# Other planning figures for the attention steps of a fused RWKV and tanh-shrink kernel

## The chip, the cores and the metric

The kernel runs on one core of a Trainium2 chip. A core has five engines that run their own instruction queues in order and wait for each other through semaphores: TensorE (PE, matrix products), VectorE (DVE), ScalarE (ACT), GpSimd (POOL) and SyncE (SP, here only for issuing transfers). The metric is the device time of one execution in microseconds; smaller is better.

## What is computed

Two blocks follow each other. The first is a linear attention with a decaying state; the second a two-layer block with the activation h - tanh(h). All numbers are 32-bit floats as the kernel computes them.

```python
for t in range(S):                       # B, H, S, D = 4, 8, 768, 48
    kt, vt, rt = k[:, :, t], v[:, :, t], r[:, :, t]
    cur = np.einsum('bhd,bhe->bhde', u[None] * kt, vt)
    y[:, :, t] = np.einsum('bhd,bhde->bhe', rt, state + cur)
    state = w[None, :, :, None] * state + np.einsum('bhd,bhe->bhde', kt, vt)
...
x = y.transpose(0, 2, 1, 3).reshape(B * S, H * D)     # 3072 x 384
h = x @ w_in                                          # w_in 384 x 2048
g = h - np.tanh(h)
return g @ w_out                                      # w_out 2048 x 384
```

## The kernel before

**Attention in units.** A unit is 64 time steps of two batches with all heads; there are 24 units, and two neighbouring units make one block of 256 tokens for the dense part (12 blocks). A unit consists of these steps, with their names in the code:

- `x.turn` and `x.turn_k` (line 763, PE): eight transposes each of r and of k into PSUM (the banks that products are written to). From unit 2 on, what is turned for k is `kw`, which DVE makes first (`x.kw`, line 894).
- `x.rT` (line 767, DVE) and `x.kT` (line 776, ACT, for later units): copies out of PSUM, r scaled by powers of the decay.
- `x.rk`, its product with `ub`, and `x.du` (lines 780, 909, 784, DVE), then `diagonal` (line 788, ACT, eight small copies): the part of each step's own key.
- `from_state` and `levels` (line 717, PE): products of rT with the state, and of rT with kT. In the first 16 units both are one planned step; in the last eight (`two`) they are two, with a tiny ACT copy `seen` (line 816) between them.
- `x.cp` (line 919, DVE): a masked copy of the levels from PSUM into `at`.
- `outputs` and `to_state` (line 717, PE): products of `at` with v, and of kw with v.
- `x.xt` and `x.rest` (line 855, ACT): copies of the result into the dense part's input, negated for every second unit; then six transfers `fill` on POOL's queue (line 876) that move the rest of the rows to their place.
- `x.add` and `x.decay` (lines 882 and 928, DVE): the new state.

**The dense part in tiles.** A tile is one block of 256 tokens and 256 of the 2048 inner columns. PE makes two halves of h (line 168, six matmul records each); ACT makes five functions of it (lines 177 to 185); DVE combines them into g (lines 192, 194, 196 and 198, the last being the masked copy that ends g). Then comes the second product. For the first 24 tiles it is taken directly (`o`, line 206); later seven products of quarter size replace eight (`p`, line 257), from sums of g that POOL makes (lines 242 to 246) and from mixed weights that DVE makes once (`mixed`, line 266). The first six blocks are taken in three passes over the inner columns (4, 4 and 8 pieces of 128), the other six each in one.

**Weights.** They arrive as 64-bit numbers in 16 pieces (line 123, on SP's and POOL's queues) and are turned into 32-bit ones by five DVE steps (lines 137, 138, 141, 142, 143) and two ACT steps (139, 140).

**What sets the order.** Nothing is issued where it stands in the source. Each step is handed to `Plan.add` with its engine, a cost in us, the steps it has to wait for, and `steps`, the number of engine instructions it stands for. `Plan.order` then looks for an order: `forward` plays all queues through with these costs, `backward` gives latest times, and a search with a fixed random seed changes due times, 2500 times with the work done by 240 us as its aim and 500 times with the whole length, and keeps what the planner finds no worse. The instructions of every engine are issued in the order of the last plan kept. In `forward`, `steps` are counted in chunks of 256 instructions, for which a load of instructions is assumed, and PE's idle time before the first dense work is filled with matmuls of the identity (line 655, `fills`), whose number follows from the planned gaps. Each change of a figure therefore moves the results of comparisons in the search, and with them the order of all queues.

The planner's figures are used for nothing else: they change neither an instruction nor what it waits for.

Of the kernel before, what the change touches and what calls it, by code (L numbers as in the profile page):

```python
# [300 lines left out]
class Plan:  # L301
# [15 lines left out]
    def add(self, engine, cost, run, after=(), due=1e9, data=0, gated=False, steps=0):  # L317
        t = SimpleNamespace(engine=engine, cost=cost, run=run, after=[x for x in after if x], due=due, data=data,
                            gated=gated, steps=steps, then=[], n=len(self.tasks))
        for x in t.after:  # L320
            x.then.append(t)
        self.tasks.append(t)
        return t
# [192 lines left out]
def near(ctx, tc, r, k, v, w, u, out, shared, moe_w_in, moe_w_out):  # L516
# [21 lines left out]
    add = plan.add  # L538
# [114 lines left out]
    def fills(to):  # L653
        def run(n):
# [6 lines left out]
    now = [add(e, 1.25 if e == "ACT" else .87, lambda e=e, at=at, x=x: e_of[e].dma_start(out=rows[at : at + NP, :, :D], in_=x.rearrange("(p i) d -> p i d", i=2)), due=-1, data=.05)  # L661
           for e, at, x in (("SP", 0, w), ("ACT", NP, u))]
# [3 lines left out]
    now = add("DVE", .45, lambda: V.tensor_scalar(  # L666
        by[:, :, 1:], wcol[:, :, None].to_broadcast([128, NP, SHORT]), W_LOW, W_HIGH, ALU.max, ALU.min), [cols])
    now = add("DVE", .7, lambda: V.tensor_tensor_scan(
        power.rearrange(flat), by.rearrange(flat), plus.rearrange(flat), 0.0, ALU.mult, ALU.add), [now])

    ups = add("ACT", .6, lambda: A.copy(w_up, power[:, :, None, :SHORT].to_broadcast([128, NP, 2, SHORT])), [now])
    now = add("DVE", 1.75, lambda: V.reciprocal(inverse, power), [now])
    inverted = now
    doubled = add("ACT", .6, lambda: A.copy(twice, inverse[:, :, None, 1:].to_broadcast([128, NP, 2, SHORT])), [now])
    now = tabled = add("PE", .7, table, [doubled], steps=8)
# [3 lines left out]
    now = add("POOL", 1.0, bounds, [keeps])  # L679
    now = add("PE", .2, lambda: T.matmul(tab[0:1, 0:1], ok[:, 0, :1], shared["one"], start=True, stop=True), [now, downs])  # L680
# [20 lines left out]
    for n in range(weights.count):  # L701
# [8 lines left out]
        now = of + ([converted[n - 2]] if n >= 2 else [])  # L710
        for name, cost in (("DVE", .47), ("DVE", .47), ("ACT", .84), ("ACT", .84), ("DVE", .87), ("DVE", .87), ("DVE", .87)):
            now = [add(name, cost, step, now)]
# [8 lines left out]
    def unit(n):  # L721
# [3 lines left out]
        ch, half = divmod(n, 2)  # L725
# [4 lines left out]
        two = n >= L * (FIRST + 2)  # L730
# [5 lines left out]
        b1, b2, b3 = (units[n - i] if n >= i else none for i in (1, 2, 3))  # L736
        x = SimpleNamespace(rest=None, rk=None, du=None, own=None)
        units.append(x)
        product = n < OWN
        swap = n >= SWAP  # L740


        direct = j == 0
# [16 lines left out]
        def turn(src, to):  # L760
            for p in range(NP):
                for z in range(2):
                    T.transpose(to[:, z, p], src[HALF[z], 2 * p : 2 * p + 2, :].rearrange("t h d -> t (h d)"), ident[HALF[z], HALF[z]])  # L763
# [22 lines left out]
        def diagonal(hs):  # L786
            for h in hs:
                A.mul(t.at[:, h % 2, h // 2], same, t.du[:, h : h + 1])  # L788
# [100 lines left out]
        free = [b1.cp, b1.diag] if n > 2 else [units[0].cp, units[0].diag] if n == 2 else []  # L889
        if two:  # L890
            free = [b1.xt, b1.rest, b1.add, b1.cp, b1.diag]
        turns, turned = .46, 16
        x.turn = add("PE", turns, lambda: turn(rt, r_ps), [x.r] + free, steps=turned)
        x.kw = add("DVE", .47, lambda: V.tensor_tensor(kw[:, :, :D], t.kt[:, :, :D], w_down, ALU.mult), [x.k, downs, b2.out])
        x.turn_k = x.rk = add("PE", turns, lambda: turn(t.kt if direct else kw, k_ps), [x.k if direct else x.kw] + free, steps=turned)
        both = [x.turn, x.turn_k]
# [6 lines left out]
        if product:  # L903
            now = add("ACT", 1.05, own_k, [x.kT, w_us])
            x.own = add("PE", .7, own_levels, [now, x.rT, b2.out], steps=64)
            x.diag = add("DVE", .64, lambda: V.copy_predicated(t.at, same.bitcast(I32)[:, None, None, :].to_broadcast([128, 2, NP, SHORT]), own_lev), [x.own, b2.out])
        else:
            x.rk = add("DVE", .47, own, [x.r, x.k, b2.du, b1.rk if not b1.own else None])
            now = add("DVE", .47, lambda: V.tensor_tensor(t.rk, t.rk, ub, ALU.mult), [x.rk, bonus])
            x.du = add("DVE", .47, own_sum, [now, b2.diag])  # L910
            now = add("ACT", 1.0, lambda: diagonal(range(0, H // 2)), [x.du, b2.out])
            x.diag = add("ACT", 1.0, lambda: diagonal(range(H // 2, H)), [now])
        begun = []
        if two:
            now = add("PE", .66, from_state, both + [x.rT, b1.xt, b1.rest, b1.add, b2.decay, x.kT], steps=64)
            begun = [add("ACT", .15, between, [now])]
        x.lev = add("PE", .7 if two else (1.33 if swap else 1.73) if ch else .7, levels,
                    begun + [x.kT, x.rT, b2.out] + ([b2.decay, b1.xt, b1.rest, b1.add] if ch else []), steps=128 if ch and not two else 64)
        x.cp = add("DVE", .64, lambda: V.copy_predicated(t.at, before, lev), [x.lev, b2.out] + ([] if product else [x.diag]))  # L919
        x.out = now = add("PE", .95 if direct else 1.21, outputs,  # L920
                          [x.cp, x.diag, x.v, b1.xt, b1.rest, b1.add] + ([x.extra] if direct else [x.kw]), steps=96 if direct else 128)
        if direct:
            now = x.out = add("PE", .55, to_state, [now, x.kw], steps=64)
        x.xt = add("ACT", .96 if swap else .4, to_xt, [now, last_h.get(j - FIRST - 2) if slot == 0 else None])
        if not direct:
            x.rest = add("ACT", .62 if swap else .26, to_rest, [x.xt] + (filled.get((j - 2, "all"), []) if slot == 0 else []))
# [95 lines left out]
    for n in range(L * (FIRST + 2)):  # L1022
        unit(n)
    mixing()
    now, done = 22.0, 0
# [7 lines left out]
    for n in range(L * (FIRST + 2), d.NU):  # L1033
        unit(n)
# [326 lines left out]
```

## Time and profile before

| what | value |
|---|---|
| median of 3 runs | 605.59 us (604.61 to 608.08) |
| the profiled execution | 607.26 us |
| span of its instructions | 605.5 us |
| PE busy | 582.4 us (96%) |
| weight loads on PE | 485.7 us (80%) |
| DVE busy | 466.4 us (77%) |
| ACT busy | 403.3 us (67%) |
| POOL busy | 201.0 us (33%) |
| largest group: h, line 168 | 1152 matmul records, 285.7 us |
| second product by seven, line 257 | 994 records in four groups, 245.4 us |
| second product, line 206 | 200 records, 74.1 us |
| transposes, line 763 | 384 matmul records for 48 turns |

The profile shows for each engine when it worked on which line, and for each idle stretch which engine or transfer ended it. An instruction's duration is not its price in a row of instructions: matmuls overlap, and so the distance from one start to the next is used where a sequence is priced. "PEclk" is the share of its full clock that PE was granted. The chain of waits in the page contains one stretch of 13 us called "issue" that begins at 73.85 us; there the chain follows the queue of POOL, while PE goes on working.

### The profile page before, as it was taken

What the parts mean: (1) busy time and instruction counts of PE and PEld (TensorE: products, weight loads), DVE (VectorE), ACT (ScalarE), POOL (GpSimd) and SP (SyncE); (2) the same over time, 40 slices, a digit from 0 to 9 for tenths busy, and PEclk for the clock granted to TensorE, in tenths of its full rate; (3) what the DMA queues carried; (4) which work ended last, traced back from release to release, by engine and by line L of the source; (5) the groups of instructions that cost most, each with busy time, mean ns of one, the idle gap of its engine ahead of it and who ended that gap; (6) DMA issues with size and microseconds to landing.
All of it is one profiled execution on the core that took longest, in us unless ns stands there. A gap on an engine that the chain in (4) does not pass through costs nothing.

```text
span 605.5 us, 14670 instructions
## 1 busy us (share of the span) xinstructions
PE 582.4 (96%) x5781; PEld 485.7 (80%) x5781; DVE 466.4 (77%) x782; ACT 403.3 (67%) x902; POOL 201.0 (33%) x366
## 2 busy tenths in 40 slices
PE   8877999999999999999999999999999999999996
PEld 4555767667777669999999999888889889889995
DVE  6699699999999999867677776767765775555666
ACT  3677699899866676655556686465866676565652
POOL 5002212021000123544455473425334435334540
PEclk9889899999999999999999999999999999999999
DMA  6966585967300210110111020122201100100101
GB/s 125 228 126 126 113 194 99 143 167 124 105 14 0 48 28 14 26 27 1 28 27 26 2 60 1 41 41 48 53 16 34 41 2 8 29 2 8 26 3 30
DMA packets 86326, 33.78 MB, mean 56 GB/s; under 512 B 78536, under 2 KB 80680, under 8 KB 86248
## 3 DMA queue, kind: packets, MB, share of 16 engines
q1 hardware_dynamic: 81084, 25.57, 21.1%
q0 software_dynamic: 4992, 6.99, 5.5%
q8 instruction: 47, 0.77, 0.5%
q14 instruction: 31, 0.25, 0.2%
q10 hardware_dynamic: 172, 0.20, 0.1%
HBM read 26.94 MB, written 4.72 MB: 52 GB/s over the span
## 4 chain that ended last, share of the span: by engine, by line
PE 76%; DVE 6%; DMA 5%; ACT 4%; issue 4%; SPq 3%; POOL 1%; DVEq 0%; ACTq 0%; POOLq 0%
PE h L168 37%; PE p L257 26%; PE o L206 6%; PE yk_ps L717 4%; SPq L750 3%; DMA st<-in_moe_w_in_dram 2%; DMA xt<-rest 1%; PE yk_ps L763 1%; POOL xt L876 1%; DMA st<-in_moe_w_out_dram 1%; DVE rT L767 1%; DVE at L919 1%; ACT s L177 1%; DVE tg L194 1%; DVE g L198 1%
## 5 line engine op out<-in xcount | busy, mean ns | idle before, releaser
L168 PE MATMUL h<-xt,w_in_sb 128*128 128x256 f32 x1152 | 285.7, 385 | 2.7 <-DMA xt<-rest 2.7
L168 PEld LDWEIGHTS h<-xt,w_in_sb 128*128 128x128 f32 x1152 | 214.6, 192 | 35.9 <-issue 2.1
L242 POOL TENSOR_TENSOR sg<-g 128x256 f32<-128x256 f32 x69 | 52.1, 755 | 176.7 <-DVE g L198 152.2
L257 PE MATMUL p<-mixed,sg 128*128 128x192 f32 x426 | 104.1, 326 | 0.0
L192 DVE TENSOR_TENSOR g<-h,th 128x512 f32<-128x512 f32 x96 | 65.8, 686 | 48.9 <-ACT s L177 23.0
L194 DVE SCALAR_TENSOR_TENSOR tg<-s,tg 128x512 f32<-128x512 f32 x96 | 71.1, 741 | 36.6 <-ACT tg L181 20.0
L181 ACT ACTIVATE tg<-h 128x512 f32<-128x512 f32 x96 | 57.2, 596 | 58.5 <-PE h L168 56.9
L179 ACT ACTIVATE th<-h 128x512 f32<-128x512 f32 x96 | 57.4, 598 | 39.1 <-PE h L168 39.0
L177 ACT ACTIVATE s<-h 128x512 f32<-128x512 f32 x96 | 57.4, 598 | 37.3 <-PE h L168 37.2
L876 POOL DMA_DIRECT2D xt<-rest x66 | 32.5, 499 | 146.3 <-ACT rest L855 145.8
L257 PEld LDWEIGHTS p<-mixed,sg 128*128 128x128 f32 x426 | 75.0, 190 | 0.3 <-issue 0.3
L198 DVE COPY_PREDICATED g<-small,tg 128x512 f32<-128x512 int32 x96 | 71.1, 741 | 4.7 <-DVE tg L196 0.5
L257 PE MATMUL p<-w_out_sb,g 128*128 128x192 f32 x284 | 71.9, 335 | 1.1 <-DVE at L919 1.1
L196 DVE SCALAR_TENSOR_TENSOR tg<-q,tg 128x512 f32<-128x512 f32 x96 | 67.5, 703 | 6.4 <-ACT q L183 2.4
L206 PE MATMUL o<-w_out_sb,g 128*128 128x384 f32 x192 | 71.3, 495 | 0.1
L183 ACT ACTIVATE q<-s,m1b 128x512 f32<-128x512 f32 x96 | 69.8, 727 | 0.6
L185 ACT ACTIVATE small<-s,smallb 128x512 f32<-128x512 f32 x96 | 69.6, 725 | 0.3
L257 PEld LDWEIGHTS p<-w_out_sb,g 128*128 128x128 f32 x284 | 51.8, 190 | 9.0 <-DVE at L919 1.5
L788 ACT ACTIVATE at<-same,du 128x64 f32<-128x64 f32 x184 | 47.9, 343 | 2.8 <-DVE du L784 2.6
L206 PEld LDWEIGHTS o<-w_out_sb,g 128*128 128x128 f32 x192 | 35.2, 190 | 15.8 <-DVE g L198 0.2
L246 POOL TENSOR_TENSOR sg<-sg,g 128x128 f32<-128x128 f32 x69 | 41.0, 594 | 5.1
L244 POOL TENSOR_TENSOR sg<-sg,g 128x128 f32<-128x128 f32 x69 | 36.6, 530 | 5.2
(133 smaller groups left out, 672.3 us busy)
## 6 DMA issues: line engine op xcount, KB each, us to landing
st<-in_moe_w_out_dram SPq DMA_DIRECT2D x8, 768.0 KB, 4.5
rt<-in_r_dram SPq DMA_DIRECT2D x48, 96.0 KB, 2.9
vt<-in_v_dram SPq DMA_DIRECT2D x48, 96.0 KB, 3.4
st<-in_moe_w_in_dram SPq DMA_DIRECT2D x16, 288.0 KB, 5.5
kt<-in_k_dram SPq DMA_DIRECT2D x44, 96.0 KB, 3.1
out_dram<-o POOLq DMA_DIRECT2D x44, 96.0 KB, 2.2
st<-in_moe_w_in_dram POOLq DMA_DIRECT2D x16, 96.0 KB, 6.0
xt<-rest POOLq DMA_DIRECT2D x66, 16.0 KB, 2.1
```

The lines of the kernel that those rows point to most:

```text
L168: self.nc.tensor.matmul(t.h2[:, z], self.w_in_sb[:, t.f // 2, kk, z * 128 : (z + 1) * 128], self.xts[t.j][:, kk].rearrange("p b t -> p (b ...
L177: A.activation(out, t.h, AF.Square)
L179: A.activation(out, t.h, AF.Tanh)
L181: A.activation(out, t.h, AF.Tanh, scale=G1)
L183: A.activation(out, t.s, AF.Square, bias=self.m1b)
L185: A.activation(out, t.s, AF.Relu, bias=self.smallb, scale=-1.0)
L192: V.tensor_tensor(t.g, t.h, t.th, ALU.subtract)
L194: V.scalar_tensor_tensor(t.tg, t.s, C4, t.tg, ALU.mult, ALU.mult)
L196: V.scalar_tensor_tensor(t.tg, t.q, K1, t.tg, ALU.add, ALU.mult)
L198: V.copy_predicated(t.g, t.small.bitcast(I32), t.tg)
L206: self.nc.tensor.matmul(self.outs[i], t.g2[:, z, i * C : (i + 1) * C], self.w_out_sb[:, t.f + z, :], start=t.first and z == 0, stop=t.last ...
L257: self.nc.tensor.matmul(ps[bank][:, half * n : (half + 1) * n], a, b, start=t.first and half == 0, stop=t.last, skip_group_check=True)
```

## The change

Seven figures in `unit`, a function in `near`, are replaced. `turned`, the number of instructions of a turn, is 8 in place of 16. The cost of `from_state` in the last eight units becomes 0.68 for 0.66, that of `levels` with `from_state` in the earlier ones 1.35 for 1.33 (1.75 for 1.73 in units that don't use `swap`), that of `outputs` with the state product 1.3 for 1.21, and that of `to_state` in the first two units 0.6 for 0.55. With the new figures the same search ends in another order on every engine.

```diff
-        turns, turned = .46, 16
+        turns, turned = .46, 8
         x.turn = add("PE", turns, lambda: turn(rt, r_ps), [x.r] + free, steps=turned)
...
-            now = add("PE", .66, from_state, both + [x.rT, b1.xt, b1.rest, b1.add, b2.decay, x.kT], steps=64)
+            now = add("PE", .68, from_state, both + [x.rT, b1.xt, b1.rest, b1.add, b2.decay, x.kT], steps=64)
             begun = [add("ACT", .15, between, [now])]
-        x.lev = add("PE", .7 if two else (1.33 if swap else 1.73) if ch else .7, levels,
+        x.lev = add("PE", .7 if two else (1.35 if swap else 1.75) if ch else .7, levels,
...
-        x.out = now = add("PE", .95 if direct else 1.21, outputs,
+        x.out = now = add("PE", .95 if direct else 1.3, outputs,
                           [x.cp, x.diag, x.v, b1.xt, b1.rest, b1.add] + ([x.extra] if direct else [x.kw]), steps=96 if direct else 128)
         if direct:
-            now = x.out = add("PE", .55, to_state, [now, x.kw], steps=64)
+            now = x.out = add("PE", .6, to_state, [now, x.kw], steps=64)
```

The beginning of PE's queue shows the kind of difference that results (number of matmuls behind the x, unit numbers added in brackets). Up to the levels of unit 1 both are the same.

```
before                                    after
levels (1) x16                            levels (1) x16
identity 512 columns x1                   identity 512 columns x3
outputs (1) x24                           outputs (1) x24
to_state (1) x16                          turn r (2) x8
turn r (2) x8                             to_state (1) x16
identity 512 x1                           turn kw (2) x8
h, first half, x3                         identity 512 x2
turn kw (2) x8                            from_state, levels (2) x32
h, second half, x3                        h, both halves, x6
from_state, levels (2) x32                outputs, to_state (2) x32
identity 512 x5                           turn r (3) x8
outputs, to_state (2) x32                 h, both halves, x6
turn r (3), turn kw (3) x16               turn kw (3) x8
h, both halves, x6                        identity 512 x1, 256 x1
from_state, levels (3) x32                from_state, levels (3) x32
```

## What is forecast, and why

> **What bounds the kernel now.** I read the page's slices first, then the busy times stage by stage, then what TensorE (PE) waited for, then the windows in which its clock fell. In the slices each digit is a fortieth of the span, 15.1 us.
>
> ```profile
> PE   8877999999999999999999999999999999999996
> DVE  6699699999999999867677776767765775555666
> PEclk9889899999999999999999999999999999999999
> ```
>
> PE is busy almost everywhere, VectorE (DVE) nearly everywhere in the first 230 us. The stages, with busy us per engine and the granted clock:
>
> ```profile
> 0.00:22.00 22.00, 16.26 (x267) 9.54 (x271) 12.62 (x28) 9.52 (x25) 9.43 (x37) 1.00 0.80 139
> 22.00:60.00 38.00, 30.82 (x580) 21.00 (x578) 35.24 (x59) 27.46 (x81) 3.94 (x8) 0.90 0.76 158
> 60.00:120.00 60.00, 57.01 (x1109) 41.75 (x1102) 52.23 (x91) 50.25 (x139) 12.20 (x24) 0.95 0.75 139
> 120.00:228.80 108.80, 106.44 (x879) 77.17 (x878) 105.84 (x173) 82.83 (x170) 11.93 (x22) 1.00 0.30 68
> 228.80:390.00 161.20, 161.20 (x957) 149.52 (x955) 120.53 (x202) 101.42 (x196) 79.65 (x131) 1.00 0.10 22
> 390.00:592.00 202.00, 201.89 (x1973) 179.78 (x1972) 132.05 (x216) 128.71 (x290) 83.86 (x145) 1.00 0.12 25
> ```
>
> Columns: PE, weight loads, DVE, ScalarE (ACT), GpSimd (POOL), clock, DMA share. From 228.8 on PE has no free time, so work can't be made faster there by another order. The losses lie before: 7.2 us of PE idle in 22 to 60, 3.0 in 60 to 120, 2.4 in 120 to 228.8. What ended them:
>
> ```profile
> PE yk_ps L717 <- DVE at L919: 3.8, 5, 1.8
> PE x_ps L763 <- DVE kw L894: 3.1, 1, 3.1
> PE h L168 <- DMA xt<-rest: 2.7, 2, 1.5
> PE yk_ps L717 <- DVE state L882: 2.2, 3, 1.1
> PE yk_ps L717 <- DVE rT L767: 1.1, 1, 1.1
> PE p L257 <- DVE at L919: 1.1, 1, 1.1
> PE x_ps L717 <- issue: 0.7, 1, 0.7
> ```
>
> Nearly all are DVE steps of attention that came late in DVE's queue. After such idle time the clock falls too:
>
> ```profile
> 22.00:26.00 4.00, 4.00 (x71) 2.87 (x66) 3.88 (x6) 1.47 (x6) 0.00 (x0) 0.59 0.99 220
> 34.00:38.00 4.00, 1.79 (x74) 1.22 (x72) 4.00 (x7) 2.80 (x7) 0.00 (x0) 1.00 0.81 150
> 38.00:42.00 4.00, 3.13 (x14) 2.57 (x15) 4.00 (x8) 2.38 (x9) 0.00 (x0) 0.62 0.66 122
> 54.00:58.00 4.00, 2.10 (x36) 1.21 (x24) 4.00 (x8) 2.31 (x9) 0.06 (x1) 1.00 0.96 145
> 58.00:62.00 4.00, 3.16 (x68) 2.65 (x69) 1.93 (x4) 2.02 (x8) 0.00 (x0) 0.68 0.80 165
> 62.00:66.00 4.00, 4.00 (x72) 2.99 (x72) 1.75 (x4) 1.09 (x2) 0.00 (x0) 0.50 0.01 1
> ```
>
> The missing clock is 4 x (0.41 + 0.38 + 0.32 + 0.50) = 6.4 us of PE time, in three dips. So some 19 us are there to win or lose before 228.8, and nothing else but new waits can be added after it.
>
> **What the Trainium skill says.** "TensorE: Matmul & The Clock Gate", What's actually happening: the default clock is half, and an idle window of about 3.4 us brings it back to half. The trace agrees in kind: 2.2 us idle in 34 to 38 is followed by 0.62, 1.9 idle in 54 to 58 by 0.68 and 0.50. "PSUM — Partial Sum Buffer", PSUM bank collisions raise a hardware error: two engines must be kept apart on one bank and quadrant, reads included. Both copies after a turn read the same banks, and in the trace rT (DVE, 0.69) started at 447.67, as kT (ACT, 447.05 + 0.58) ended. "Runtime: NRT & Kernel Launch", Instruction fetch mechanics: instructions arrive in blocks of 256 and the crossing is mostly hidden; the trace has one PE wait of 0.7 put to issue.
>
> **The change part by part.** No instruction is added or taken away but one warming matmul pair (29 units of 256 columns for 30); seven figures that only the planner reads differ. Its search draws the same random numbers, accepts other ones, and all queues come out in another order.
>
> *The figures themselves.* Start to start at 446 to 453 us the trace has a turn 0.39 (figure 0.46, kept), from_state 0.59 (0.66 to 0.68), levels 0.63 (0.70 kept), outputs with the state product 0.96 (1.21 to 1.30). So they move away from the bare times, towards a price that includes the dearer first matmul after a switch (an h half shows 1.49 instead of 1.29 in the chain). A turn has 8 matmul and 8 load records, so 16 was its count and 8 is too few: the plan puts fetch crossings too late. The price is at most the one such wait, 0.7; I take 0, since the order up to it (lev of unit 1, at 18.1) is the same.
>
> *Start, up to unit 4.* I laid the built orders of both side by side and summed durations of the DVE instructions ahead of each attention mask copy (L919), by distances from start to start: L137, L138, L780, L894, L909, L784 0.47 each, L141, L142, L143 0.87, L192, L194, L196, L767 0.60, L919 and L198 0.63. Unit 1: L919 now stands ahead of the conversion's L137, which waited 2.9 us for weights; PE sat 1.8 us. Three warming pairs now fill this gap: they end at 18.5 + 6 x 0.44 = 21.2 against 21.43, so 0.2 is won, and a clock dip perhaps. Unit 2: kw (L894) and rT come ahead of L143, its chain starts at once; DVE has to finish at 31.0 (weights conversion waits for ACT's L140 at about 30.1), +0.7 for L919, outputs at 31.7 against 34.38: 2.7 won. Both have done one h tile by then. Unit 3: L138, L143, L192 and L196 are gone from before its L919 (2.5 us). Its h tile stands before the turn of kw and waits for L143 at about 34.3, ends at 37.0; kT to 38.2, rT to 39.1, L919 41.0 to 41.7: outputs 41.8 against 46.21, 4.4 won. Unit 4: first half of the o tile waits for L198 at 45.9 (2 us idle on PE, new), L919 at 49.0 to 49.7: outputs 49.8 against 53.14. Lead 3.3, with the same dense work done (2 h tiles, 1 o tile). SP's loads keep their sequence to here but for one vt half and the w_out pieces, shifted by one load of 0.65; kt of unit 4 landed at 37.3 and is wanted at 39.
>
> *The next h tile* waits for the six fills on POOL's queue. They follow rest of unit 3, on ACT at 45.7 by the same sums against 50.08, and the landing took 6.2 us with a weight load in front, 2.1 as median. In the new order that weight load stands eight places later in SP's queue. I take 2.0 of the 2.7 us wait and of its 3.3 us of missing clock together (ends 0 and 6).
>
> *60 to 228.8.* By the same sums DVE has 7 to 10 us less ahead of the L198 of tiles 8 to 23, because units 12 and 13 are put off (unit 12's outputs from 38 to 84 us of dense PE work) and conversions come later. That is cover, not gain: the o tiles are bound by PE here (L198 done 20 us early). Against it, the mixed weights (L266) move 9 us back on DVE, to 198 + 18 = 216 us (18 is DVE's offset in the trace at this point), wanted by the first p at about 230. In the burst of units 12 to 15 rT of unit 13 has 174.6 us of DVE work before it: with this offset 192.7, while PE wants it at about 189. I count 0, ends -4 and +4.
>
> *228.8 to the end.* The same PE work. The distances inside units 16 to 23 get tighter: between levels and outputs seven of eight units have one piece of PE work of 1.0 to 1.3 us (before: two), between turn and from_state three have 1.0 to 1.3 (before: one). The one before shows what this costs when DVE is ready: outputs started 0.55 us after L919 had ended, and from_state 0.1 late. I take 10 x 0.07 = -0.7; if DVE is one instruction (0.6) late at each, -6. The last tile: two ACT steps change place, no p waits for them; 0.
>
> Sum: 3.3 + 2.0 + 0 - 0.7 = 4.6 us won. The profiled execution took 607.26 (its span of 605.50 and 1.76 around it), so its like would take 602.7. The median of the runs shown is 605.59, that is 1.67 lower; from it: 601.0.
>
> **The rivals.** A, the forecast: the early lead stays; 601.0, chance 0.50. B: the lead is waited away at the burst of units 12 to 15, where DVE's queue is the second bound. For it: DVE 105.84 of 108.8 us. Against: it has 20 us of cover on the o tiles. 4.6 - 4 = 0.6 won, 605.0; chance 0.22. C, slower: the tight units 16 to 23. Place: L919 and L767 in the p stage; price 0.6 a miss, ten misses 6, on top of a lead of only 2 from the start: 605.6 - 2 + 6 = 609.6. It decides from about eight misses. Against: DVE is busy only 65% there. Chance 0.15. D, slower: the new 2 us of idle before the first o half puts the clock to half for some 6 us (as at 58 to 66: 3.3 lost), and the fills land as late as before: 3.3 - 3.3 - 0 - 0.7, and up to 2 more of waits by later kw: 606.3 to 608.3, say 607.3; chance 0.13.
>
> **How the numbers follow.** Within 0.5% of 605.59 is 602.6 to 608.6, about what a measurement of this kernel can tell from no change. Of A 0.49 lies under 602.6 and 0.01 in between; B gives 0.06 faster, 0.14 same, 0.02 slower; C 0.01 same and 0.14 slower; D 0.07 same, 0.06 slower. Faster 0.55, same 0.23, slower 0.22. The range holds A's ends (lead 3.3 with fills at 6 and burst at +1: 595.5) and most of C, to 609.5; A's own is 596 to 603.
>
> **What would show it.** Right: outputs of unit 2, 3 and 4 at about 31.7, 41.8 and 49.8; no PE wait for kw (L894) of 3 us; clock dips in 22 to 70 worth less than 5 us; PE idle in 22 to 60 under 5; first p not later than the extra dense work before it explains; under 1 us of PE idle after 240. Wrong: PE waits for rT or state near 190; PE waits for L919 or L767 in 390 to 592; a new dip at 46 to 55. The step I trust least is the fills' landing.

## The result, and the profile after

| | before | after |
|---|---|---|
| median of 20 runs each, us | 606.41 (602.16 to 609.25) | 603.21 (601.12 to 607.24) |
| ratio, 95% interval | | 0.9947 (0.9931 to 0.9963) |
| the profiled execution, us | 607.26 | 601.73 |
| its span, us | 605.5 | 600.0 |
| its mean granted clock of TensorE | 0.989 | 0.995 |

The change makes the kernel 0.5% faster. The two profiled executions stand 5.5 us apart, the medians 3.2: the profiled execution of before was one of its longer ones, that of after one of the shorter. What is read below from two traces is therefore larger than what the change is worth on average, by a factor of up to 1.7. Two executions of one edited kernel, the one with warming matmuls, ran in a slower state (612.17 and 613.18 us); its ratio and its mean clock loss leave them out.

The slices of the page of after, a fortieth of 600 us each:

```profile
PE   8888989999999989999999999999999999999996
DVE  5799969999999999986777775665776775555765
PEclk9899999999999999999999999999999999999999
```

The third and fourth slice of PE, 30 to 60 us, show 8 in place of 7, and the clock has one digit under 9 where before had three. The stages by windows (PE, weight loads, DVE, ACT, POOL, clock, DMA share, GB/s):

```profile
0.00:22.00 22.00, 19.38 (x312) 11.22 (x315) 12.70 (x28) 8.81 (x25) 9.14 (x37) 1.00 0.81 142
22.00:60.00 38.00, 31.37 (x604) 21.87 (x594) 36.29 (x62) 31.93 (x89) 4.35 (x8) 0.96 0.80 158
60.00:120.00 60.00, 56.25 (x1076) 40.31 (x1076) 52.88 (x92) 51.70 (x139) 14.75 (x30) 1.00 0.81 146
120.00:228.80 108.80, 107.00 (x936) 79.23 (x935) 107.09 (x176) 86.46 (x176) 11.34 (x19) 1.00 0.27 64
228.80:390.00 161.20, 160.29 (x980) 148.23 (x979) 122.43 (x206) 97.70 (x200) 82.00 (x133) 1.00 0.12 26
...
22.00:26.00 4.00, 1.63 (x41) 1.23 (x32) 3.22 (x6) 1.61 (x3) 0.00 (x0) 0.81 1.12 161
26.00:30.00 4.00, 4.00 (x70) 2.07 (x69) 3.75 (x8) 4.00 (x15) 0.00 (x0) 0.76 1.05 343
...
58.00:62.00 4.00, 4.00 (x91) 3.27 (x90) 4.00 (x8) 3.86 (x10) 0.00 (x0) 1.00 0.62 124
62.00:66.00 4.00, 3.88 (x73) 2.43 (x72) 3.58 (x8) 3.92 (x13) 2.60 (x6) 1.00 0.59 105
```

From 22 to 60 us PE stands idle 6.6 us, hardly less than before's 7.2. What has changed is the clock: 0.96 for 0.90 there, 1.00 for 0.95 in the next stage. One dip is left, at 22 to 30, and takes 4 x (0.19 + 0.24) = 1.7 us; before had three that took 6.4. From 58 to 66, where before had 0.68 and 0.50, after has 1.00. And DVE did 1.05 us more work in 22 to 60 and 1.25 us more in 120 to 228.8, where it is as good as full in both kernels. The waits of PE in after:

```profile
PE x_ps L763 <- DVE kw L894: 2.4, 1, 2.4
PE yk_ps L717 <- DVE state L882: 2.2, 3, 0.9
PE o L206 <- DVE g L198: 1.9, 1, 1.9
...
PE x_ps L763 <- DVE at L919: 1.2, 1, 1.2
PE h L168 <- DMA xt<-rest: 1.1, 1, 1.1
```

The wait for kw is still there, but for unit 2 (at 24.7) instead of unit 3. The wait before the first o half (1.9, at 44.5 to 46.4) is new, as forecast. That for the fills went from 2.7 to 1.1.

Where the time was won shows best as a *lead*: each matmul record of PE's dense and attention work is given one price, the same in both traces; these prices are added up in order of time, and where both sums are equal the time of the other kernel is subtracted from that of before. Warming matmuls count nothing. The columns stand at before's time; positive is ahead of before.

| kernel | 47.0 | 54.5 | 67.4 | 103.1 | 137.6 | 208.5 | 271.3 | 591.2 |
|---|---|---|---|---|---|---|---|---|
| after | 4.0 | 2.7 | 7.7 | 6.9 | 8.7 | 8.5 | 5.7 | 5.6 |
| early part after's, rest before's | 3.6 | 2.3 | 7.0 | 5.4 | 5.4 | 5.4 | 5.4 | 5.4 |
| early part before's, rest after's | -1.2 | -1.3 | -1.1 | -3.5 | -1.7 | -1.8 | -4.5 | -4.7 |
| warming matmuls added to before | -1.0 | -2.2 | 0.7 | 0.7 | -3.1 | -3.1 | -3.1 | -3.1 |
| before, kw of unit 3 ahead | 0.9 | 0.4 | 1.9 | 1.9 | 1.9 | 1.9 | 1.9 | 1.9 |
| the same, mask copy of unit 3 ahead too | 1.4 | -1.9 | 3.6 | 3.3 | 3.3 | 3.3 | 3.2 | 3.2 |
| after, two moves in unit 2 | 3.4 | 2.1 | 7.3 | 6.7 | 8.5 | 8.4 | 5.7 | 5.5 |
| the same, three moves more at 205 to 250 | 3.5 | 2.3 | 7.3 | 6.2 | 8.0 | 7.8 | 4.4 | 4.2 |
| cut at 100 | 3.9 | 1.0 | 7.0 | 6.0 | 0.6 | 0.6 | 0.6 | 0.6 |
| cut at 75, with the moves in unit 2 | 3.7 | 0.9 | 7.1 | 1.8 | 1.8 | 1.8 | 1.8 | 1.8 |

In after 2.7 us are won up to the outputs of unit 4, 5.0 at the next h tile, about 1 more by 140, and 2.8 are lost between 205 and 265. The second of these is the largest. The timeline of before shows it, PE from the first wait for the fills on:

```profile
56.98 0.67 PE L168 MATMUL h<-xt,w_in_sb 128*128 128x256 f32 x2 [1.55 <-DMA xt<-rest]
58.84 0.67 PE L168 MATMUL h<-xt,w_in_sb 128*128 128x256 f32 x2 [1.19 <-DMA xt<-rest]
59.44 1.10 PE L717 MATMUL yk_ps<-rT,state 48*48 48x64 f32 x32
...
61.33 2.92 PE L168 MATMUL h<-xt,w_in_sb 128*128 128x256 f32 x6
64.19 1.11 PE L717 MATMUL yk_ps<-at,vt 64*48 64x64 f32 x32
```

The same in after:

```profile
53.81 2.43 PE L168 MATMUL h<-xt,w_in_sb 128*128 128x256 f32 x10 [1.11 <-DMA xt<-rest]
56.17 0.67 PE L717 MATMUL yk_ps<-rT,state 48*48 48x64 f32 x32
...
57.23 2.86 PE L168 MATMUL h<-xt,w_in_sb 128*128 128x256 f32 x12
60.02 0.66 PE L717 MATMUL yk_ps<-at,vt 64*48 64x64 f32 x32
```

Six records of h take 2.92 us in before, twelve take 2.86 in after; the attention products take 1.10 and 0.66. PE counts as busy throughout, so no view of idle time shows this loss. What the wait for the fills lost less (2.7 - 1.1 = 1.6 us) and the clock that isn't missing at 58 to 66 (3.3 us) make 4.9 of these 5.0 us.

### The profile page after: what moved, and what is told of

Read it like the earlier page. It is cut to its first block, busy times and chain, and to the rows that moved or that the text cites. A ratio compares the mean times of both kernels' runs of the same rounds, so it can differ in the third digit from the quotient of the medians.

```text
span 600.0 us, 14634 instructions
## 1 busy us (share of the span) xinstructions
PE 579.3 (97%) x5781; PEld 482.5 (80%) x5781; DVE 467.1 (78%) x782; ACT 403.3 (67%) x902; POOL 203.4 (34%) x366
## 4 chain that ended last, share of the span: by engine, by line
PE 70%; DVE 13%; ACT 6%; DMA 5%; issue 3%; SPq 1%; POOL 0%; DVEq 0%; ACTq 0%; POOLq 0%
PE h L168 34%; PE p L257 25%; PE o L206 5%; PE yk_ps L717 4%; DMA kt<-in_k_dram 2%; DMA xt<-rest 1%; DMA st<-in_moe_w_in_dram 1%; DVE g L198 1%; DVE tg L196 1%; SPq L750 1%; DVE tg L194 1%; ACT at L788 1%; DVE g L192 1%; PE yk_ps L763 1%; DVE mixed L266 1%
## 5 line engine op out<-in xcount | busy, mean ns | idle before, releaser
L168 PE MATMUL h<-xt,w_in_sb 128*128 128x256 f32 x1152 | 283.1, 383 | 2.6 <-DMA xt<-rest 1.1
L168 PEld LDWEIGHTS h<-xt,w_in_sb 128*128 128x128 f32 x1152 | 212.4, 190 | 34.5 <-DMA xt<-rest 1.5
L194 DVE SCALAR_TENSOR_TENSOR tg<-s,tg 128x512 f32<-128x512 f32 x96 | 68.6, 715 | 52.9 <-ACT tg L181 28.1
L192 DVE TENSOR_TENSOR g<-h,th 128x512 f32<-128x512 f32 x96 | 65.5, 683 | 28.0 <-ACT s L177 11.1
L177 ACT ACTIVATE s<-h 128x512 f32<-128x512 f32 x96 | 57.4, 598 | 41.8 <-PE h L168 41.5
L198 DVE COPY_PREDICATED g<-small,tg 128x512 f32<-128x512 int32 x96 | 75.2, 784 | 4.4 <-DVE tg L196 0.5
L196 DVE SCALAR_TENSOR_TENSOR tg<-q,tg 128x512 f32<-128x512 f32 x96 | 68.0, 708 | 9.8 <-ACT q L183 7.4
L206 PE MATMUL o<-w_out_sb,g 128*128 128x384 f32 x192 | 70.2, 492 | 2.3 <-DVE g L198 1.9
L206 PEld LDWEIGHTS o<-w_out_sb,g 128*128 128x128 f32 x192 | 35.4, 190 | 19.3 <-issue 2.2
L244 POOL TENSOR_TENSOR sg<-sg,g 128x128 f32<-128x128 f32 x69 | 43.2, 626 | 5.1
L246 POOL TENSOR_TENSOR sg<-sg,g 128x128 f32<-128x128 f32 x69 | 36.9, 535 | 5.1
```

Source lines behind the costliest of these rows:

```text
L168: self.nc.tensor.matmul(t.h2[:, z], self.w_in_sb[:, t.f // 2, kk, z * 128 : (z + 1) * 128], self.xts[t.j][:, kk].rearrange("p b t -> p (b ...
L177: A.activation(out, t.h, AF.Square)
L192: V.tensor_tensor(t.g, t.h, t.th, ALU.subtract)
L194: V.scalar_tensor_tensor(t.tg, t.s, C4, t.tg, ALU.mult, ALU.mult)
L196: V.scalar_tensor_tensor(t.tg, t.q, K1, t.tg, ALU.add, ALU.mult)
L198: V.copy_predicated(t.g, t.small.bitcast(I32), t.tg)
```

## Experiments

All kernels but those with another seed issue the steps from a list of numbers written into the kernel, so that the order can be edited; with the list of after it is after's order exactly:

```diff
-    for t in plan.order():
...
-        t.run()
+    for word in ORDER.split():
...
+            plan.tasks[int(word)].run()
```

The list shifts the line numbers: 32 are added in attention (L717 becomes L749, L763 L795, L882 L914, L919 L951) and 81 in the dense part (L168 becomes L249, L192 L273, L198 L279, L206 L287).

### Which part of the order: the early one or the rest?

Two lists: the steps that one plan places before 70 us in its order, then all others in the order of the other plan.

```diff
+ORDER = (steps of after planned before 70) + (the other steps in before's order)
+ORDER = (steps of before planned before 70) + (the other steps in after's order)
```

> Every queue follows the changed kernel's order for the steps planned before 70 us, and the order of before for the rest. Theory of the start (the lead is won in the first 70 us and PE carries it on): at least the net gain of the changed kernel, ratio to before 0.987 to 0.993, since the units 12 to 15 are not put off and the loss at 205 to 265 us (2.9 us) doesn't come back. Theory of the middle (the gain comes from putting off units 12 and 13 and the conversions): ratio 0.997 to 1.003.

> The other way round: before's order for the steps planned before 70 us, the changed kernel's for the rest. Theory of the start: no lead, and the waits at 205 to 265 us that the changed order has: ratio 1.000 to 1.005. Theory of the middle: the changed kernel's gain, ratio 0.993 to 0.996.

The first measured 602.59 us against 605.75, ratio 0.9946 (0.9928 to 0.9964): the whole gain of the change, 0.9947, comes with its first 70 us. Its lead stays at 5.4 us once before's order has taken over. The second measured 611.06, 1.0085 (1.0054 to 1.0115). It says less, because it loses 2.6 us right behind the cut and, in the profiled execution, has a wait of 3.1 us inside the levels of unit 1, which no edit touched. The profile calls such a wait "issue": PE waited for nothing that the profile shows. Where the text below says that PE waited for its own instructions, this is meant; that they were being fetched is not shown.

```profile
PE x_ps L749 <- issue: 3.1, 1, 3.1
PE x_ps L795 <- DVE kw L926: 3.1, 1, 3.1
PE o L287 <- DVE g L279: 2.6, 1, 2.6
```

But it shows that the loss between 205 and 265 belongs to after's order of those steps: with another start it is there again, from -1.8 to -4.5, and with before's order it isn't.

### Are the new figures better, or is it another draw?

The search of the planner is seeded. Both sets of figures were given other seeds.

```diff
-        chance = Random(5)
+        chance = Random(6)
```

> The old figures with another seed of the planner's search (6 for 5); nothing else. Theory of the draw (any change to the search gives another order, good or bad by chance): anywhere within 0.990 to 1.012, no likelier near 1 than the changed kernel. Theory of the figures (the new ones plan better): within 0.998 to 1.004 of before.

> The new figures with seed 6. Theory of the draw: anywhere within 0.990 to 1.012, with no order relative to the old figures with seed 6. Theory of the figures: 0.992 to 0.997, faster than the old figures with seed 6 by about 0.5%.

> The new figures with a third seed of the planner's search, 7. Theory of the figures (the new ones give a better order than the old ones): again near after, 601 to 604, 0.3 to 0.8% faster than before. Theory of the draw (any change of a figure or of the seed draws another order; two draws of the old figures gave 1 and 0.9964, two of the new ones 0.9947 and 1.0016): anything within about 0.6% of before on either side, 602 to 609; only a value over 605 tells the two apart.

| seed | old figures | new figures |
|---|---|---|
| 5 | 1 (before) | 0.9947 (0.9931 to 0.9963) |
| 6 | 0.9964 (0.9944 to 0.9983) | 1.0016 (0.9998 to 1.0034) |
| 7 | | 1.0007 (0.9993 to 1.0022) |

With seed 6 the sign is reversed (602.81 us with the old figures, 606.81 with the new), and with 7 the new figures are not faster than before either; the old ones were not run with 7. That the figures as such make plans better by the 0.5% seen is contradicted, and the change is a draw that came out well. Five draws can't exclude a much smaller effect. The old figures with seed 6 are worth a look: in the profiled execution PE stood 3.8 and 2.7 us for nothing but its own instructions, and the kernel was faster than before all the same.

```profile
PE x_ps L717 <- issue: 3.8, 1, 3.8
PE yk_ps L717 <- DVE at L919: 2.8, 3, 1.8
PE x_ps L763 <- issue: 2.7, 1, 2.7
```

### What binds the start: PE's waits, its clock, or DVE's queue?

Three edits of before's order; numbers in brackets are units. In the first, warming matmuls fill two gaps of PE:

```diff
 levels (1)
+identity 512 columns x2
 outputs (1)
...
 turn r (3)
+identity 512 columns x3
 turn kw (3)
```

> The order of before, unchanged but for five more warming matmuls of 512 columns, written into a buffer that is idle there: two ahead of the outputs of unit 1, three ahead of the turn of kw of unit 3. They stand in gaps in which PE waited 1.8 and 3.1 us in before. Theory of the clock (the early lead comes from dips that no longer happen): the dips at 22 to 26 (0.59) and 38 to 42 (0.62) vanish, 1.6 + 1.5 us are won, 602 to 603.5. Theory of the DVE queue (the start is bound by what stands ahead of attention's copies on DVE; the clock only follows): the dips vanish, but the outputs of units 2, 3 and 4 start where they did, within 0.5 us (34.4, 46.2, 53.1), and the time is within 1 us of before.

It measured 608.09, ratio 1.0024 (1.0003 to 1.0044), slightly slower. The windows at the second gap (38 to 42 had 0.62 in before) and at the h tile behind the fills:

```profile
38.00:42.00 4.00, 3.67 (x18) 1.96 (x18) 4.00 (x8) 1.40 (x6) 0.00 (x0) 1.00 0.72 134
54.00:58.00 4.00, 2.56 (x80) 2.28 (x80) 3.97 (x7) 3.48 (x12) 1.53 (x4) 0.61 0.72 160
58.00:62.00 4.00, 3.14 (x26) 2.16 (x30) 2.98 (x6) 1.72 (x8) 0.00 (x0) 0.53 0.65 120
```

PE's timeline, outputs of units 3 and 4:

```profile
47.17 0.67 PE L749 MATMUL yk_ps<-at,vt 64*48 64x64 f32 x32 [0.77 <-DVE at L951]
...
54.60 0.87 PE L749 MATMUL yk_ps<-at,vt 64*48 64x64 f32 x32 [1.30 <-DVE at L951]
```

The dip at 38 to 42 is gone, and little or nothing is won by it: outputs of unit 3 start at 47.17 (46.21 in before) and now wait for DVE, which is busy 4.00 of 4.00 us at 38 to 42. The dip at 22 to 26 only became smaller (0.73): PE waited 2.1 us for its own instructions inside the levels of unit 1 in this execution, and the warming matmuls then stood in front of the outputs of unit 1 (24.51 for 21.43). That late start blurs the comparison, but between the outputs of unit 2 (35.95, in before 34.38) and those of unit 3 the kernel made up only 0.6 us on before, not the 1.5 us that the dip at 38 to 42 had taken. The clock that is missing while DVE has no free time cost little here. The dips at 54 to 62 stayed, and from 58 on DVE isn't full (2.98 of 4; in before 1.93 and 1.75 in the two windows from 58 to 66). That the warming matmuls made the kernel 0.24% slower was foreseen by neither theory; in the profiled execution, one of the longer ones, 4 us were lost between 110 and 125 us, where PE waited 1.7 us for its own instructions inside an o half and its clock then fell to 0.50. Whether the warming matmuls bring that about is open.

The second and third edit move steps of unit 3 on DVE, the third on top of the second:

```diff
+L780, L894 (3)
 L142
...
 L137
-L780, L894 (3)
```
```diff
+L928, L919 (3)
 L143
 L780, L894, L909 (4)
-L928, L919 (3)
```

> The order of before, with the product of r and k and kw of unit 3 (L780, L894 of before) moved four places ahead on DVE, in front of L142, so that kw is ready at about 35 us instead of 38.8. Theory of the PE waits (a wait is worth its length): the wait of 3.1 us for kw goes, outputs of unit 3 start 2.5 to 3 us earlier than 46.2, and about 3 us are won. Theory of the DVE queue: the mask copy L919 of unit 3 has the same work ahead of it on DVE as in before, so it ends at 45.6 as before, outputs start at 46.2, the wait only moves to it, and the time is within 1 us of before.

> As the kernel that moves kw of unit 3 ahead, and in addition the decay and the mask copy of unit 3 (L928 and L919 of before) moved ahead of L143 and of unit 4's L780, L894 and L909 on DVE. Theory of the DVE queue: the copy ends at about 42.3, outputs of unit 3 start at 42.4 to 43.2 instead of 46.2, and 2 to 3 us of lead stay to the end unless L143 or kw of unit 4, now later, is waited for. Theory of the PE waits: no more than the 3 us that moving kw alone gives. A third possibility: DVE is full from 22 to 60 in both, so that the wait returns at the next h or o tile (L198 of the first tile and kw of unit 4) and under 1 us is won.

Moving kw alone gave 605.18, ratio 0.9993 (0.9976 to 1.0009); with the mask copy as well 604.43, 0.9979 (0.9964 to 0.9993). PE's timeline of the first:

```profile
37.32 2.83 PE L249 MATMUL h<-xt,w_in_sb 128*128 128x256 f32 x12 [1.59 <-DVE w_in_sb L224]
41.90 0.67 PE L749 MATMUL yk_ps<-rT,state 48*48 48x64 f32 x32 [1.75 <-DVE state L914]
...
45.28 0.66 PE L749 MATMUL yk_ps<-at,vt 64*48 64x64 f32 x32 [0.77 <-DVE at L951]
```

The wait of 3.1 us for kw has become three: 1.59 for the converted weights, 1.75 for the state, 0.77 for the mask copy, together 4.1. The outputs start 0.9 us earlier. The move in DVE's full queue didn't remove PE's wait, it passed it on to the next steps. With the mask copy ahead, outputs of unit 3 started at 44.84, not at 42.4 to 43.2: the levels ahead of it still waited 1.75 us for the state, which the estimate had left out. The theory of the DVE queue holds in kind; of the 2 to 3 us that it promised for the mask copy, about half came (1.3 to 1.5).

### Can after be mended at its own wait for kw?

Two moves on DVE in after's order:

```diff
+L894 (2)
 L141
 L780 (2)
-L894 (2)
...
+L919 (2)
 L141
-L919 (2)
```

> The order of after with two moves on DVE: kw of unit 2 (L894) ahead of the conversion's L141, into the 1.3 us in which DVE waited for ACT, and the mask copy of unit 2 (L919) ahead of the next L141. PE waited 2.4 us for that kw, at 24.7, and its clock was 0.81 and 0.76 in 22 to 30. Theory of the PE waits and the clock: the wait and the dip go, 2.4 + 1.7 = 4 us are won against after, about 599. Theory of the DVE queue: all DVE work of the start remains, and only about 1 us of DVE's idle time is used, so outputs of units 3 and 4 start 0.5 to 1.4 us earlier than 42.2 and 50.4 and 0.5 to 1.4 us are won against after, 601.5 to 603.

602.61, ratio 0.9919 (0.9897 to 0.9942); its interval meets that of after, and the spans of the two profiled executions are 600.1 and 600.0. PE's timeline:

```profile
19.66 0.45 PE L749 MATMUL x_ps<-rT,kT 48*64 48x64 f32 x12 [1.91 <-issue]
...
24.32 0.71 PE L749 MATMUL yk_ps<-at,vt 64*64 64x64 f32 x24
...
32.36 0.67 PE L749 MATMUL yk_ps<-at,vt 64*48 64x64 f32 x32
```

The wait for kw is gone, but in this execution PE waited 1.9 us for its own instructions inside the levels of unit 1, and the outputs of unit 1 started 3.8 us later than in after (20.53). The outputs of unit 2 started at 32.36 all the same, in after at 32.37: the delay used up what the wait for kw had been. Two later kernels have the same two moves and were not delayed at unit 1 (the first of the next part started its outputs at 20.62). There PE waited 0.4 and 1.0 us for kw, and then 2.3 and 1.6 us in front of the levels of unit 2, for ACT's copies of the diagonal (L820). The outputs of unit 3 started at 42.84, 42.68 and 42.54 in the three kernels with the moves, and at 42.24 in after. Wherever PE's waits lie before unit 3 in these four executions, they move its outputs by no more than 0.6 us: 2.4 to 3.8 us of PE time are free there. The theory of the PE waits, 4 us won against after, is contradicted. Whether the 0.5 to 1.4 us came that the other theory allowed is open: the medians differ by 0.6 us and the ratios by 1.7, with intervals that meet, and at the outputs of units 3 and 4 the traces show nothing won.

### Are the 3 us at 205 to 265 to be had?

After's lead stands at 8.4 at before's 227 us and at 5.8 at 265. PE's timeline of after shows three waits in that amount of work, that of before one:

```profile
211.44 0.46 PE L763 MATMUL x_ps<-ident,rt 64*128 64x64 f32 x8 [1.24 <-DVE at L919]
220.86 0.66 PE L717 MATMUL yk_ps<-rT,state 48*48 48x64 f32 x32 [0.56 <-DVE state L882]
249.31 1.56 PE L168 MATMUL h<-xt,w_in_sb 128*128 128x256 f32 x6 [0.71 <-DVE g L192]
```

And before:

```profile
226.99 0.59 PE L257 MATMUL p<-w_out_sb,g 128*128 128x192 f32 x2 [1.12 <-DVE at L919]
```

In after the mask copy of unit 14 stands behind a step that mixes weights (L266) and one of the dense part; the turn of unit 15, which needs the same PSUM, waited for it 1.24 us. DVE's timeline of after:

```profile
209.08 0.81 DVE L266 TENSOR_TENSOR mixed<-w_out_sb 128x384 f32<-128x384 f32 x1
209.81 0.94 DVE L196 SCALAR_TENSOR_TENSOR tg<-q,tg 128x512 f32<-128x512 f32 x1
210.67 0.71 DVE L919 COPY_PREDICATED at<-before,x_ps 128x512 f32<-128x512 int32 x1
```

```diff
+L919 (14)
 L266
 L196
-L919 (14)
...
+L882 (14)
 L194
...
-L882 (14)
...
+L192
 L780
 L194
-L192
```

> The order of after with the two moves of unit 2, and three more on DVE where after lost lead at 205 to 265 us: the mask copy L919 of unit 14 ahead of one mixing of weights and one L196 (PE waited 1.24 us for it at 211.4), the state copy L882 of unit 14 ahead of an L194, an L196 and two mixings (0.56 at 220.9), and an L192 ahead of an L780 and an L194 (0.71 at 249.3). Theory of the place (attention's copies stand behind mixing work that has time): the three waits go, nothing new comes, 1.5 to 2.5 us are won against the kernel with the moves of unit 2 alone, span 597.5 to 598.6, about 600.5. Theory of the full DVE queue (107 of 108.8 us busy in 120 to 228.8): the work put behind is wanted in turn by the next L198 and the first p, the waits return there, under 0.7 us is won, 602 or more.

604.35, ratio 0.9983 (0.9961 to 1.0005); the lead ends at 4.2, 1.3 under that without these three moves. PE's timeline behind 212 us:

```profile
220.69 0.66 PE L749 MATMUL yk_ps<-rT,state 48*48 48x64 f32 x32 [1.04 <-DVE state L914]
...
239.54 1.56 PE L249 MATMUL h<-xt,w_in_sb 128*128 128x256 f32 x6 [0.85 <-DVE g L273]
...
245.06 1.56 PE L249 MATMUL h<-xt,w_in_sb 128*128 128x256 f32 x6 [0.39 <-DVE g L273]
```

The wait of 1.24 went, and the lead was 9.1 at before's 227 us, against 8.4. Then it came back: 1.04 for the state (0.56 before the moves), 0.85 and 0.39 for g. One of the three moves was bad by itself: L882 was put so early that DVE stood 0.8 us for ACT's copy `rest` of the same products. DVE is full there, 23.59 of 23.8 us from 205 to 228.8 in after and 9.62 of 10 from 240 to 250. So the theory of the full queue has the better of it, but a better placing isn't excluded.

Two further cuts asked whether after's lead of 8 us is partly DVE work put off, to be paid later:

```diff
+ORDER = (steps of after planned before 100) + (the other steps in before's order)
+ORDER = (steps of after planned before 75, with the two moves of unit 2) + (the other steps in before's order)
```

> The order of after for all steps planned before 100 us, and the order of before for the rest (the earlier one of this kind was cut at 70 us and kept a lead of 5.4 us, while after had 8 at 70 to 200 us and lost 3 at 205 to 265). Theory of the middle (the 3 us are lost by the order after 100 us, in which units 12 and 13 come late and crowd before the products by seven): the lead is 6 to 8 us at equal PE work and stays, span 597.5 to 600. Rival theory (the lead of 8 is partly dense work done ahead of attention steps, a debt that is paid in any order): the lead falls to 5 to 5.5 once before's order has caught up with the steps that were put off, span about 600 to 601.

> The order of after for the steps planned before 75 us, with the two moves of unit 2 as in the kernel that has these alone, and the order of before for the rest. At this cut the sets of steps done differ by nothing in the sum of PE's planned cost and by 0.3 us in that of DVE's (at 100 us DVE had 4.3 us less behind it, and that kernel lost its lead right after the cut). Theory of the debt on DVE (after's lead of 8 us at 70 to 200 us is paid for with DVE work put off, 3 us of it fall due at 205 to 265): here nothing is put off, so the lead after the cut, 5.5 to 8 us, stays to the end: span 597 to 600. Rival (any cut costs what was won on the way): the lead falls to 4 or less by 120 us, span 601 to 603.

They measured 606.7, 1.0021 (1.0002 to 1.004), and 605.05, 0.9971 (0.9953 to 0.999); the spans, 604.8 and 603.8 us, are longer than any of the theories had said. Both lose 5 to 6 us right behind the cut, the one at 100 by a single wait of 4.0 us for L198 and a clock of 0.89 between 90 and 120 us, the one at 75 by the following waits and a clock of 0.50 between 86 and 90. Its PE timeline:

```profile
83.00 0.66 PE L749 MATMUL yk_ps<-rT,state 48*48 48x64 f32 x32 [1.88 <-DVE state L914]
...
85.78 1.10 PE L749 MATMUL yk_ps<-at,vt 64*48 64x64 f32 x32 [1.65 <-DVE at L951]
```

At 75 no DVE work was owed in the sum, and the lead fell all the same. So these two don't show a debt; they show that a seam between two plans can have a cost of its own, here 5 us; the cut at 70 lost 1.6. Whether part of the lead of 8 us was borrowed is left open.

### The clock, run by run

Each timed execution comes with its mean granted clock. The clock times lost, (1 - clock) x span, average 6.3 us in 203 executions of before (mean clock 0.9896) and 3.5 us in 20 of after (0.9941). Over the 203 the time follows the loss with a correlation of 0.86, 0.76 us for each us lost. For the difference of 2.7 us in this loss that makes 2.1 of the 2.7 us by which the mean times differ (606.05 and 603.33). It is a correlation: idle time that comes before a dip is counted with it, so the clock alone is probably worth less than 2.1. Of the edited kernels, the one with the mask copy of unit 3 ahead fits: 3.3 us lost, 1.5 us won, though in its trace the outputs of unit 3 start 1.4 us earlier and those of unit 4 1.1 us later than in before. But the clock isn't all: the old figures with seed 6 lose 7.4 us and are faster than before, and the kernel with warming matmuls loses 5.3, less than before, and is slower.

The dip at the h tile behind the fills goes with the order of the start. In all five traces that begin in before's order (before, warming matmuls, the two with moves in unit 3, before's early part with after's rest) the clock fell to between 0.50 and 0.57 in a window of 4 us between 54 and 66; in all six that begin in after's order it was 1.00 in all three windows there. No run takes the dip away and leaves the rest of before's start as it is, for instance with warming matmuls in the wait for the fills. So what the clock alone is worth at this place is read from the traces, not shown by an experiment.

## Why the prediction was right or wrong

The forecast was 601.0 us and faster; 603.21 was measured, within the range, and faster. On the scale of the profiled run it was 4.6 us won, and 5.5 were seen. Measured from the median of 20, 606.41, the same 4.6 would have led to 601.8: the median gain of 3.2 is 0.7 of what was forecast. That the sum met the profiled run is luck in part: one term was 3.0 too small, another took 2.1 more than it was given, and the two offset each other.

- **The figures themselves, 0.** Nothing speaks against it. But a price of "at most 0.7" for a fetch wait was too low: in executions with an identical PE queue up to there, the one wait inside the levels of unit 1 was between 0 and 3.1 us.
- **Start to unit 4, 3.3.** Outputs of units 1 to 4 were forecast at 21.2, 31.7, 41.8 and 49.8 and started at 20.53, 32.37, 42.24 and 50.41; 2.7 us were won at the last. The method, summing DVE's durations ahead of each mask copy, is right within 0.7 us at each unit, and the kernels with two moves in unit 2 show why it can work without looking at PE at all. That PE would wait 2.4 us for kw of unit 2 was missed, and didn't matter. "PE idle in 22 to 60 under 5" was wrong with 6.6, for the same reason: the idle time there isn't the loss.
- **The next h tile, 2.0 (0 to 6).** The mis-sized term: 5.0. The fills started at 46.67 in place of 50.12 and the last of them landed at 53.77 (before 58.71), the wait fell by 1.6, and the dip at 58 to 66 (3.3 us) went altogether. The prediction had both sizes, 2.7 and 3.3, and took a third of their sum. That the two follow from the fills, as it said, fits the traces; how they share the 5.0 no experiment shows.
- **60 to 228.8, 0.** The lead rose from 7.7 at the end of that h tile to 8.7 and stood at 8.4 at before's 227. The loss was sought at rT of unit 13 near 190; the first new wait came 20 us later, 1.24 us at the mask copy of unit 14, behind L266 and L196, and before's own wait of 1.12 in front of its first p makes up for it. The mixed weights did no other harm up to there: the first p started at 226.95, in before at 226.99, with more of the other work done.
- **228.8 to the end, -0.7.** -2.8, the second mis-sized term. After these 227 us of before the lead fell to 5.8 at 265: 0.56 for the state, 0.71 for g, and two pauses of 0.3 and 0.2 us. "PE has no free time" there was true of before; in after PE was idle 1.1 us behind 240, where under 1 had been named as a sign of being right. Together with the stage before, this is rival B in kind: part of the lead is waited away on a full DVE queue. It is B's size only in part (2.8 of 4), it comes later than B said, and it is taken from a lead of 8.5. From 265 on 0.2 are lost. In units 16 to 23 the outputs started 0.06 to 0.56 us after the mask copy in seven of eight, without a gap on PE, and PE was idle 0.23 us in 390 to 592. The misses of rival C didn't come.
- **Rival D, the clock after the new idle time.** The idle stretch came as foreseen (1.88 us), and in after the clock stayed at 1.00. The rival was no phantom: with nearly the same start and the same idle stretch it fell to 0.58 and to 0.70 in the two kernels cut at 100 and 75. The window of the first:

```profile
46.00:50.00 4.00, 3.50 (x36) 1.85 (x40) 3.38 (x7) 1.85 (x8) 2.91 (x6) 0.58 0.80 150
```

What the prediction lacked as a whole is the order of importance. It built the gain on earlier attention steps and added the clock as an uncertain extra; by the traces, the earlier steps matter because they bring the fills forward to where PE is the bound, and there, in these two traces, the clock that stays warm is 3.3 of the 5.0 us. One sum is off by a little: its lowest end, fills at 6 and burst at +1, comes to 596.0, not 595.5.

## What to carry to other kernels

A wait of PE need not be worth its length where another engine is full in that stretch: here 2.4 to 3.8 us of PE time before unit 3 could come and go with at most 0.6 us of effect on its outputs, while the 3.3 us of clock missing at 58 to 66, where DVE was busy 1.93 and 1.75 of 4 us, seem by the leads to have been paid in full. So price a stage by the queue that is full in it, and look for cold matmuls (the same row of six at 2.92 instead of 1.5 us) as well as for idle time. And where a searched plan follows from figures, compare several seeds of old and new figures before crediting the figures: the draws here spread over 0.7%.

## What was not expected of the hardware

- The same 1.87 to 1.88 us of PE idle before the first o half was followed by a clock of 1.00 in four kernels and of 0.58 and 0.70 in two. "TensorE: Matmul & The Clock Gate" of the Trainium skill (What's actually happening) says that the activity window runs freely and that results therefore vary from run to run; these traces agree. Its idle window of about 3.4 us is not a lower limit in them: single idle stretches of 1.9 us (the two cut kernels) and 2.4 us (after, at 22.4 to 24.7) were followed by a dip. The 2.2 us in 34 to 38 that the prediction names are a window's share; that wait was 3.1 us long.
- Waits for instructions in one place vary between executions of an equal PE queue: 0.72 in before, none in after, and 0.7, 0.7, 1.9, 2.1, 2.1, 2.7 and 3.1 us in seven of the edited kernels, each inside the levels of unit 1; two more had 0.2 and none. The profile names nothing that these waits were for. "Runtime: NRT & Kernel Launch" (Instruction fetch mechanics) calls the crossing from one block of instructions to the next mostly hidden. If these waits are such crossings, which no run here shows, at this early place it mostly wasn't.
